# Down projection by Strassen's identity and softmax of two head groups at once, in a two-layer attention and GeGLU kernel

## The chip, the cores and the metric

The kernel runs on one core of a Trainium2 chip. A core has five engines that run their own instruction lists and meet at semaphores: TensorE (PE) for matrix products, with its weight loads (PEld) beside them, VectorE (DVE), ScalarE (ACT), GpSimd (POOL), and SyncE (SP), which here issues all DMA transfers. Matrix products land in PSUM, everything else is in SBUF. The metric is the time of one execution on the device in microseconds (us), the median of several runs.

## The reference

Two layers, each with the same weights: a dilated sliding-window attention and a GeGLU feed-forward network, both behind a layer norm and with a residual. Sequence S = 2048, width D = 512, 32 heads of 16, window W = 8 at dilation 2, F = 1792, all in float32.

```python
x = A_x
x = x + _A_ref(_layernorm(x), A_wqkv, A_wo)        # attention
x = x + _B_ref(_layernorm(x), w_gate, w_up, w_down)
x = x + _A_ref(_layernorm(x), A_wqkv, A_wo)
x = x + _B_ref(_layernorm(x), w_gate, w_up, w_down)

# attention: position p sees p, p-2, ..., p-14 of its own head
logits = einsum("bhsd,bhswd->bhsw", q, kg) * Dh**-0.5   # masked where p - 2w < 0
o = einsum("bhsw,bhswd->bhsd", softmax(logits), vg)
# feed-forward
y = (gelu(x @ w_gate) * (x @ w_up)) @ w_down
```

## The kernel before

Rows are split by parity, since a window of dilation 2 stays within one parity. A chunk is 256 rows of one parity, kept as J = 2 row tiles of 128; there are eight chunks a layer. For each chunk `attention_inputs` normalizes the rows and projects them to q, k and v (in two halves h of the heads, two row tiles j: four pieces of 24 matmuls, line 905), moves each piece from PSUM to a staging tile (line 925) and stores it to a DRAM tensor qkvd. `attention` fetches q, k and v back, with a halo of seven earlier rows so that a window is a shift along the free dimension, for four head groups of eight heads. Per head group VectorE multiplies the window of k by q (line 981), sums each product over 16 elements to logits (988), takes the softmax (1010 to 1034, exponential on ScalarE), multiplies the window of v by the weights in two instructions (1040) and adds the eight window places in a tree (1051 twice, 1056). `feed_forward` projects the result by wo, adds the residual, normalizes, and runs seven units u of two F blocks each: gate and up on TensorE into a PSUM tile pg (871), gelu on ScalarE (1141), product on VectorE (1149, called the eviction here: it frees the pg tile), and then the down projection (1174) into a PSUM tile pd.

Products of float32 are made of float16 halves: each operand is split into a high part and a remainder (`split`, `split_transpose`; the remainder of the gate product is GpSimd's line 1163, the cast ScalarE's 1158), and `passes` multiplies high by high, high by remainder and remainder by high. So each product is three matmuls. Weights are scaled by powers of two, which come from their largest absolute values (537, 547), before they are split (498 on VectorE, 514 and 518 on ScalarE and GpSimd).

The order of the work is laid out before the program is emitted. Every step is a node of a `Graph` with an engine, an estimated time, its reads and writes, and a priority; `plan` simulates the engines and takes the node that can start soonest, ties by priority. The priorities are built from the table of numbers `AT`. A `Lease` is the use of one buffer of a `Pool`; a node that gets a lease waits until a buffer is free. Before, pg has three buffers of two PSUM banks, pd one of two banks, the staging tiles three of their own. Once planned, each engine's list is fixed, and an engine that waits holds up everything behind it.

## Time and profile before

| what | us |
|---|---|
| median of 3 runs (lowest to highest) | 1263.62 (1263.05 to 1264.64) |
| span of the profiled execution, first to last instruction | 1259.6 |
| TensorE busy | 1229.9 (98%) |
| VectorE busy | 989.2 (79%) |
| ScalarE busy | 497.6 (40%) |
| GpSimd busy | 415.5 (33%) |

The page gives the profiled execution's span and no other time of its own; the span lies 4.0 us under the median of the runs. Busy time is the time in which an engine has an instruction under way. A group row of the profile has the line, the engine, the operation, output <- inputs, the shapes and the count, then the busy time in us and the mean of one in ns, then the engine's idle time ahead of such instructions and what ended it. A row of the chain or of the timeline has start and duration in us. A row of the table of windows has the window and its length, the busy time of each engine with its instructions, the granted TensorE clock (1.00 is full), the busy share of the DMA engines and GB/s.

### The profile page before, as it was taken

How to read it: one execution, taken by the hardware profiler on the slowest of the kernel's cores; microseconds unless marked ns; L12 is line 12 of the kernel's file. 1: busy time of each engine (PE TensorE's matmuls, PEld its weight loads, DVE VectorE, ACT ScalarE, POOL GpSimd, SP SyncE). 2: the span in 40 equal slices, each digit the busy share in tenths (PEclk: the TensorE clock that was granted, in tenths of full speed). 3: DMA queues.
4: the chain of work that ended last, by engine and by line, in shares of the span. 5: the costliest groups of instructions: out<-in, count | busy, mean ns of one | idle time of the engine just before them, and what ended most of it. 6: DMA issues, size and time to landing. Idle time of an engine off the chain costs nothing.

```text
span 1259.6 us, 21521 instructions
## 1 busy us (share of the span) xinstructions
PE 1229.9 (98%) x8714; PEld 854.8 (68%) x8714; DVE 989.2 (79%) x1422; ACT 497.6 (40%) x754; POOL 415.5 (33%) x405
## 2 busy tenths in 40 slices
PE   6988999999999999999999999999999999999998
PEld 3654585767767676767666667667676667776775
DVE  7989888988888889889888988688898888952011
ACT  6856383433434334343333343233343333321211
POOL 3523455252524243434233242332311314231211
PEclk8998999999999999999999999999999999999999
DMA  9999724735544543645282562835454463210000
GB/s 314 328 309 258 199 93 116 218 91 141 153 116 145 141 129 112 182 109 156 70 234 78 153 165 84 202 82 122 134 145 153 119 187 103 71 43 35 18 18 17
DMA packets 195779, 174.59 MB, mean 139 GB/s; under 512 B 101904, under 2 KB 162656, under 8 KB 195680
## 3 DMA queue, kind: packets, MB, share of 16 engines
q1 hardware_dynamic: 195680, 173.23, 48.3%
q8 instruction: 68, 1.11, 0.4%
q14 instruction: 31, 0.25, 0.1%
HBM read 115.87 MB, written 33.73 MB: 119 GB/s over the span
## 4 chain that ended last, share of the span: by engine, by line
PE 89%; DMA 4%; DVE 2%; ACT 2%; POOL 1%; SPq 1%; issue 1%; POOLq 0%; DVEq 0%; ACTq 0%
PE pg L871 52%; PE pd L1174 22%; PE pg L905 15%; DMA ax<-hl 2%; DMA bx<-hl 1%; DMA x<-in_A_x_dram 1%; DVE prod L1040 0%; SPq L834 0%; ACT w_q L493 0%; DMA qkvd<-stg 0%; DMA xa<-in_A_x_dram 0%; ACT xn L860 0%; POOL hl L829 0%; DVE prod L1051 0%; DMA ot<-hl 0%
## 5 line engine op out<-in xcount | busy, mean ns | idle before, releaser
L871 PE MATMUL pg<-bx,w_g 128*128 128x256 f16 x2688 | 330.1, 273 | 0.4 <-DMA bx<-hl 0.4
L871 PE MATMUL pg<-bx,w_u 128*128 128x256 f16 x2688 | 330.0, 273 | 0.0
L1163 POOL TENSOR_TENSOR gh<-g,gh 128x512 f16<-128x512 f32 x112 | 165.4, 1476 | 444.4 <-ACT gh L1158 425.1
L1174 PE MATMUL pd<-w_d,gh 128*128 128x512 f16 x1344 | 304.6, 379 | 0.6 <-POOL gh L1163 0.6
L871 PEld LDWEIGHTS <-w_g 128*128 128x128 f16 x2688 | 262.8, 98 | 47.2 <-issue 0.5
L871 PEld LDWEIGHTS <-w_u 128*128 128x128 f16 x2688 | 263.0, 98 | 30.5
L905 PE MATMUL pg<-w_q,ax 128*128 128x512 f16 (+1 forms) x1536 | 260.8, 331 | 16.5 <-DMA ax<-hl 12.4
L905 PEld LDWEIGHTS <-ax 128*128 128x128 f16 x1536 | 151.7, 99 | 124.0 <-DMA ax<-hl 12.9
L1174 PEld LDWEIGHTS <-gh 128*128 128x128 f16 x1344 | 131.5, 98 | 143.5 <-POOL gh L1163 1.0
L1149 DVE SCALAR_TENSOR_TENSOR g<-pg,small,g 128x512 f32<-128x512 f32 (+1 forms) x128 | 85.8, 681 | 169.3 <-ACT g L1141 164.3
L1141 ACT ACTIVATE g<-pg,small 128x512 f32<-128x512 f32 (+1 forms) x128 | 79.5, 634 | 267.6 <-PE pg L871 262.1
L1040 DVE TENSOR_TENSOR prod<-v,lg 128x1024 f32<-128x1024 f32 x128 | 168.0, 1338 | 1.1
L981 DVE TENSOR_TENSOR prod<-k,q 128x2048 f32<-128x2048 f32 x64 | 152.5, 2382 | 0.9
L1051 DVE TENSOR_TENSOR prod<-prod 128x1024 f32<-128x1024 f32 (+1 forms) x128 | 148.2, 1158 | 2.5
L988 DVE TENSOR_REDUCE lg<-prod 128x128 f32<-128x2048 f32 x64 | 145.9, 2280 | 1.0
L829 POOL TENSOR_TENSOR hl<-xn,hl 128x512 f16<-128x512 f32 x64 | 91.9, 1446 | 152.7 <-ACT hl L825 152.6
L829 POOL TENSOR_TENSOR hl<-o,hl 128x256 f16<-128x256 f32 x64 | 68.7, 1074 | 184.4 <-ACT hl L825 173.2
L1158 ACT CAST gh<-g 128x512 f16<-128x512 f32 x112 | 68.9, 616 | 85.5 <-DVE g L1149 83.1
L925 ACT ACTIVATE stg<-pg 128x768 f32<-128x768 f32 x64 | 51.8, 810 | 109.2 <-PE pg L905 107.3
L871 PE MATMUL pg<-w_o,ot 128*128 128x512 f16 x384 | 85.7, 379 | 0.1
L1141 ACT ACT_TABLE_LOAD x42 | 53.9, 1283 | 61.9 <-PE pg L871 61.5
L871 PEld LDWEIGHTS <-ot 128*128 128x128 f16 x384 | 37.5, 98 | 42.7 <-DMA ot<-hl 0.6
(84 smaller groups left out, 715.1 us busy)
## 6 DMA issues: line engine op xcount, KB each, us to landing
k<-qkvd SPq DMA_DIRECT2D x64, 576.0 KB, 4.4
v<-qkvd SPq DMA_DIRECT2D x64, 576.0 KB, 3.7
qkvd<-stg SPq DMA_DIRECT2D x64, 384.0 KB, 3.5
q<-qkvd SPq DMA_DIRECT2D x64, 128.0 KB, 2.1
x<-in_A_x_dram SPq DMA_DIRECT2D x9, 512.0 KB, 5.3
xs<-x SPq DMA_DIRECT2D x8, 512.0 KB, 3.8
xa<-xs SPq DMA_DIRECT2D x16, 256.0 KB, 6.2
x<-xs SPq DMA_DIRECT2D x8, 512.0 KB, 4.9
```

Source lines behind the costliest of these rows:

```text
L829: "POOL", t_pool(n), lambda: nc.gpsimd.tensor_sub(lo(), src(), hi()),
L871: nc.tensor.matmul(pt, a, b, start=i == 0, stop=i == n - 1)
L905: nc.tensor.matmul(pt[:, lo:hi], a[:, i // 2, kt], part(h * KT + kt)[:, lo:hi], start=(i, kt) == (0, 0), stop=(i, kt) == (2, KT - 1),)
L981: nc.vector.tensor_mul(pr, win, q.tile()[:, 0:J].unsqueeze(2).to_broadcast([P, J, W, P]))
L988: lambda lgv=lgv: nc.vector.tensor_reduce(lgv(), pr.rearrange("p j w (h d) -> p j w h d", d=DH), axis=AX.X, op=ALU.add),
L1040: lambda j=j, v=v, lg=lg: nc.vector.tensor_mul(prod[:, j].rearrange("p w (h d) -> p w h d", d=DH), v.tile()[:, j : j + W].rearrange("p w ( ...
L1051: lambda a=a, b=b: nc.vector.tensor_add(pr[:, :, 0:a], pr[:, :, 0:a], pr[:, :, a:b]),
L1141: lambda sel=sel, h=h, pg=pg, gt=gt: nc.scalar.activation(gt.tile()[:, sel, 0:N], pg.tile()[:, sel, 0:N], AF.Gelu_apprx_tanh, scale=cst["s ...
L1149: lambda sel=sel, h=h, pg=pg, gt=gt: nc.vector.scalar_tensor_tensor(gt.tile()[:, sel, 0:N], pg.tile()[:, sel, JM * P : JM * P + N], cst["c ...
L1158: lambda gt=gt, gh=gh: nc.scalar.copy(gh.tile()[:, 0, :, 0:N], gt.tile()[:, :, 0:N]),
L1163: lambda gt=gt, gh=gh: nc.gpsimd.tensor_sub(gh.tile()[:, 1, :, 0:N], gt.tile()[:, :, 0:N], gh.tile()[:, 0, :, 0:N]),
L1174: nc.tensor.matmul(pd.tile()[:, j], gh.tile()[:, a, i, cs], wd_of(f, b), start=f == 0 and n == 0, stop=f == NF - 1 and n == 2,)
```

## The change

The down projection takes a 2 x 2 x 2 block form: the two row tiles of a chunk, the two F blocks of a unit, and the two halves of D. Strassen's identity computes it with seven block products in place of eight, each 128 x 128 by 128 x 256, in three passes. For that the seven combinations of the gate blocks are made for every unit (`sums` on GpSimd), then cast and split, and the seven combinations of the w_down blocks are made once at the start (`finish`: sums and remainder on VectorE, cast on ScalarE). The seven products are accumulated over all units in seven blocks of 256 columns of a pd tile that is now four banks, and six VectorE instructions gather them into the rows. With pd grown, pg has two buffers of two banks; the two further ones that lie in pd's banks are withdrawn at the very start. Softmax is taken over two head groups in one instruction each; the weighted v is one multiplication and one reduction over the window, read with a stride of 128 elements, in place of two multiplications and the tree. The norm ahead of the feed-forward moves from VectorE's to GpSimd's form. Staging tiles, gate tiles, normalized rows and scratch share one pool sc of three buffers; k and v share one of three. The table of priorities is new.

On VectorE, around the first evictions of gate tiles (g in before, sc in after). In before:

```order
L1040 TENSOR_TENSOR prod<-v_108,lg_112 128x1024
L1051 TENSOR_TENSOR prod<-prod 128x2x512
L1051 TENSOR_TENSOR prod<-prod 128x2x256
L1056 TENSOR_TENSOR o_116<-prod 128x256
L1149 SCALAR_TENSOR_TENSOR g_117<-pg_126,small,g_117 128x512
L981 TENSOR_TENSOR prod<-k_105,q_109 128x2048
L1149 SCALAR_TENSOR_TENSOR g_118<-pg_128,small,g_118 128x512
```

and in after, where L703 to L706 are the sums and L728 the remainders of w_down:

```order
L1176 TENSOR_REDUCE o_112<-prod 128x256
L728 TENSOR_TENSOR w_d<-w_d 128x1792
L703 TENSOR_TENSOR sc_101<-sc_101 128x128
L704 TENSOR_TENSOR sc_101<-sc_101 128x256
L705 TENSOR_TENSOR sc_101<-sc_101 128x128
L706 TENSOR_TENSOR sc_101<-sc_101 128x128
L1275 SCALAR_TENSOR_TENSOR sc_102<-pg_122,small,sc_102 128x512
L1166 TENSOR_TENSOR prod<-kv_105,lg_109 128x2048
L1176 TENSOR_REDUCE o_112<-prod 128x256
L728 TENSOR_TENSOR w_d<-bx_96,w_d 128x7x128
L728 TENSOR_TENSOR w_d<-sc_100,w_d 128x7x128
L1275 SCALAR_TENSOR_TENSOR sc_102<-pg_123,small,sc_102 128x512
```

The w_down preparation, which was GpSimd's and ScalarE's, stands between attention and the first evictions.

On SyncE's queue, where the first chunk's q and k are fetched from qkvd. In before:

```order
L531 DMA w_u<-in_B_w_up_dram 128x896
L531 DMA w_g<-in_B_w_gate_dram 128x896
L936 DMA qkvd_64<-stg_104 128x6x128
L963 DMA q_109<-qkvd_64 128x256
L963 DMA q_110<-qkvd_64 128x256
```

and in after:

```order
L555 DMA w_u<-in_B_w_up_dram 128x896
L555 DMA w_d<-in_B_w_down_dram 128x512 x12
L831 DMA xa_89<-in_A_x_dram 128x512
L831 DMA xa_87<-in_A_x_dram 128x512
L788 DMA qkvd_65<-zeros 12x7x128 x2
L831 DMA xa_88<-in_A_x_dram 128x512
L1077 DMA q_106<-qkvd_64 128x256
```

Twelve of the fourteen w_down loads now stand ahead of the first fetch; in before all stood behind it.

On the same queue, the stores of projections shortly ahead of the first gate/up in after (stg_102, stg_103 and stg_104 took turns in before):

```order
L1047 DMA qkvd_64<-sc_102 128x6x128 x2
L831 DMA xa_88<-in_A_x_dram 128x512
L940 DMA_TRANSPOSE ax_92<-hl_99 128x8x128
L940 DMA_TRANSPOSE ax_94<-hl_98 128x8x128
L1047 DMA qkvd_64<-sc_102 128x6x128
L1077 DMA kv_105<-qkvd_64 128x1152
L1047 DMA qkvd_64<-sc_102 128x6x128
L940 DMA_TRANSPOSE ot_97<-hl_99 128x4x128
L1047 DMA qkvd_64<-sc_102 128x6x128
```

Thirteen stores in a row leave from the one buffer sc_102, while w_down's preparation and the gate tiles hold the others.

The diff, cut to its core:

```diff
 AT = dict(
-    lq0=-1380.0, lq1=-908.3, lf0=-0.8, lo=20.4, lf1=59.8, ld=93.7, pq0=-1380.0, pq1=-275.7, pf0=10.5, po=1.8,
...
+    lq0=-6486.17, lq1=-3733.04, lf0=-475.32, lo=-1195.16, lf1=-292.25, ld=-286.77, pq0=-1258.2, pq1=2564.18,
...
-    P_pg = pool("pg", 3, [P, 2, 512], F32, ps, fifo=False)
-    P_pd = pool("pd", 1, [P, JM, 512], F32, ps)
+    pd_all = ps.tile([P, 8, HD], F32, name="pd")
+    pd_two = pd_all.rearrange("p (t b m) c -> p t b (m c)", t=2, b=2)
+    P_pg = Pool("pg", [ps.tile([P, 2, 512], F32, name=f"pg{i}") for i in range(2)] + [pd_two[:, i] for i in range(2)], fifo=False)
+    P_pd = Pool("pd", [pd_all])
...
-    P_st = pool("stg", 3, [P, 3, HH, P])
...
+    P_sc = pool("sc", 3, [P, 7 * P], fifo=False)
...
+        def sums(b):
+            tt = (nc.gpsimd if AT["ds"] else nc.vector).tensor_tensor
+            tt(b[:, 0], b[:, 3], b[:, 6], op=ALU.add)
+            tt(b[:, 1:3], b[:, 3:7:2], b[:, 4:7:2], op=ALU.add)
+            tt(b[:, 4], b[:, 4], b[:, 6], op=ALU.subtract)
+            tt(b[:, 5], b[:, 5], b[:, 3], op=ALU.subtract)
...
+                lambda: g.add("ACT", t_act(7 * n), lambda: nc.scalar.copy(hi, blocks()), **rest[0]),
+                lambda: g.add(
+                    "POOL" if AT["dl"] else "DVE port", t_pool(7 * n) if AT["dl"] else t_dve(7 * n),
+                    lambda: sub(lo, blocks(), hi), **rest[1],
+                ),
...
+                def av(v=v, lg=lg, heads=heads):
+                    r = v.tile()[:, 0]
+                    win = bass.AP(r.tensor, r.offset, [r.ap[0], [P, J], [P, W], [DH, HPG], [1, DH]])
+                    nc.vector.tensor_mul(
+                        prod.rearrange("p j w (h d) -> p j w h d", d=DH), win,
+                        lg.tile()[:, :, :, heads].unsqueeze(4).to_broadcast([P, J, W, HPG, DH]),
+                    )
...
+                    lambda o=o: nc.vector.tensor_reduce(
+                        o.tile(), prod.rearrange("p j w c -> p j c w"), axis=AX.X, op=ALU.add
                     ),
...
-            for a, b in ((4, 8), (2, 4)):
-                g.add(
-                    "DVE port", t_dve(J * a * P),
-                    lambda a=a, b=b: nc.vector.tensor_add(pr[:, :, 0:a], pr[:, :, 0:a], pr[:, :, a:b]),
...
-        nl, sb_of = norm(xt, T - 1000)
-        bx = Lease(P_bx)
+        nl, sb_of = norm(xt, T - 1000, "POOL" if AT["fp"] else "DVE")
+        bx = Lease(P_bx, only=c % 2)
...
+                tt = nc.gpsimd.tensor_tensor if AT["sp"] else nc.vector.tensor_tensor
+                tt(b[:, 4:6], b[:, 0:2], b[:, 3:4].to_broadcast([P, 2, P]), op=ALU.add)
+                tt(b[:, 6], b[:, 0], b[:, 2], op=ALU.add)
+                tt(b[:, 1:3], b[:, 1:3], b[:, 0:4:3], op=ALU.subtract)
...
-                            nc.tensor.matmul(
-                                pd.tile()[:, j], gh.tile()[:, a, i, cs], wd_of(f, b),
-                                start=f == 0 and n == 0, stop=f == NF - 1 and n == 2,
-                            )
...
+                for m in ms:
+                    for n, (a, b) in enumerate(((0, True), (0, False), (1, True))):
+                        nc.tensor.matmul(
+                            pd.tile()[:, PD_AT[m]], gh_of()[:, a, G_AT[m]], wd_of(u, m, b),
+                            start=u == 0 and n == 0 and PD_AT[m] % 2 == 0,
+                            stop=u == NU - 1 and n == 2, skip_group_check=True,
+                        )
...
+        for to, of, sign in (
+            ((1, 2), (5, 4), 1), ((0, 3), (4, 3), 1), ((0, 3), (5, 2), -1), ((1, 2), (3, 2), 1),
+            ((0, 3), (7, 6), 1), ((0, 3), (1, 1), 1),
+        ):
```

More of the change, by code (lines that the diff above doesn't have):

```diff
@@ L1064, in attention @@
         return ot, mark
-    ts_ = {"store": None}
     def feed_forward(l, c, T, ot, mark):
@@ L1070, in feed_forward @@
         N = J * P
+        last = l == 1 and c == len(CHUNKS[l]) - 1
         xt, xl = load_x(l, c, T - AT["xl"], order=[mark])
@@ L1194, in feed_forward @@
-        last = l == 1 and c == len(CHUNKS[l]) - 1
+                "DVE", t_dvp(D), gather, r=[(pd, m) for m in {*of}], w=[(xl, j) for j in range(J)], prio=T - 2500,
+            )
         for js in [slice(j, j + 1) for j in range(J)] if last else [slice(0, J)]:
```

443 lines of the change are left out of this document (274 added, 169 removed).

## The prediction

> **What bounds the kernel now.** I read the busy shares and the chain that ended last first, then the same shares cut at the moment the first gate/up projection starts (154.5 us, a row of the chain further down).
>
> ```profile
> PE 1229.9 (98%) x8714; PEld 854.8 (68%) x8714; DVE 989.2 (79%) x1422; ACT 497.6 (40%) x754; POOL 415.5 (33%) x405
> PE 89%; DMA 4%; DVE 2%; ACT 2%; POOL 1%; SPq 1%; issue 1%; POOLq 0%; DVEq 0%; ACTq 0%
> ...
> core 0: us, PE busy (x) PEld busy (x) DVE busy (x) ACT busy (x) POOL busy (x), PEclk, DMA share, GB/s
> 0.00:52.53 52.53, 40.74 (x227) 23.76 (x228) 40.50 (x86) 38.20 (x58) 23.21 (x61) 0.94 0.94 321
> 0.00:154.47 154.47, 130.31 (x748) 75.66 (x749) 133.16 (x229) 93.65 (x151) 56.79 (x106) 0.93 0.95 283
> 154.47:1200.00 1045.53, 1044.97 (x7565) 739.80 (x7564) 847.85 (x1182) 394.71 (x588) 350.60 (x292) 1.00 0.44 124
> ```
>
> TensorE carries 89% of the chain. From 154.5 to 1200 us it is idle for 0.6 us of 1045.5 at full clock, so there the time is TensorE's list of work and nothing else. Before 154.5 us it idles 24 us and runs at a granted clock of 0.93, while VectorE (133 of 154 us) and the DMA engines (95%) are the full ones. So I make two sums: when the stream of gate/up projections begins, and how much TensorE work is left from there.
>
> What TensorE pays per matmul is read from unbroken pieces of the chain, not from the mean of one in the groups, since matmuls overlap.
>
> ```profile
> 154.47 15.72 PE pg L871 x144
> ...
> 280.94 5.18 PE pd L1174 x24
> ...
> 291.36 7.80 PE pg L905 x48
> 299.16 5.24 PE pg L871 x48
> ```
>
> A 256-column matmul takes 5.24/48 = 109.2 ns, a 512-column one 5.18/24 = 215.8 ns. The third piece (24 of each) confirms both: 24 x 0.325 = 7.80. After 154.5 us, 1259.6 - 154.5 = 1105.1 us follow.
>
> **The change part by part.** *Down projection.* Per pair of F blocks, 12 matmuls of 512 columns become 7 products x 3 passes = 21 of 256: 12 x 0.2158 = 2.59 us becomes 21 x 0.1092 = 2.29 us. Gate/up already runs one weight load and 256 columns per matmul, so the new form has a price in the trace. 16 chunks x 7 pairs x 0.297 = **-33.3 us**, all of it on TensorE's path. (The eighth product that Strassen saves is 12.5%; a 256-column matmul costs 1.2% more than half a 512-column one.) The Trainium skill ("TensorE: Matmul & The Clock Gate", Back-to-back issue gap) says streams of load-and-matmul pairs are spaced at about 131 ns for 512 columns and 81 ns for 128; by that, halving columns would lose: 1344 x 0.131 = 176 us before against at least 2352 x 0.081 = 191 us after, slower by 15 us or more. The rows above (215.8 and 109.2 ns) contradict it, so it gets no chance.
>
> *Order of TensorE.* 96 projection matmuls (four pieces of 3.9 us, 15.6 us) move ahead of the first gate/up. The total is the same; left from the first gate/up on are 1105.1 - 33.3 - 15.6 = 1056.2 us in before's terms, its tail included.
>
> *VectorE ahead of the first eviction.* There are only two gate/up buffers (pg) instead of three, so the third gate/up waits for the first eviction (L1149, now L1275). Before, it began here:
>
> ```profile
> 52.53 2.28 DVE L981 TENSOR_TENSOR prod<-k,q 128x2048 f32<-128x2048 f32 x1
> ...
> 160.47 0.75 DVE L1149 SCALAR_TENSOR_TENSOR g<-pg,small,g 128x512 f32<-128x512 f32 x1 [0.51 <-ACT g L1141]
> ...
> L1040 DVE TENSOR_TENSOR prod<-v,lg 128x1024 f32<-128x1024 f32 x128 | 168.0, 1338 | 1.1
> L981 DVE TENSOR_TENSOR prod<-k,q 128x2048 f32<-128x2048 f32 x64 | 152.5, 2382 | 0.9
> L988 DVE TENSOR_REDUCE lg<-prod 128x128 f32<-128x2048 f32 x64 | 145.9, 2280 | 1.0
> L1051 DVE TENSOR_TENSOR prod<-prod 128x1024 f32<-128x1024 f32 x64 | 90.1, 1408 | 1.1
> ...
> L1051 DVE TENSOR_TENSOR prod<-prod 128x512 f32<-128x512 f32 x64 | 58.1, 907 | 1.3
> L1056 DVE TENSOR_TENSOR o<-prod 128x256 f32<-128x256 f32 x64 | 32.6, 509 | 10.2 <-POOL hl L829 6.8
> ...
> L1010 DVE TENSOR_REDUCE mx<-lg 128x16 f32<-128x128 f32 x64 | 23.8, 372 | 0.8
> L1187 DVE SCALAR_TENSOR_TENSOR x<-pd,small,x 128x512 f32<-128x512 f32 x32 | 22.5, 746 | 19.2 <-PE pd L1174 19.2
> ...
> L1034 DVE TENSOR_TENSOR lg<-lg,mx 128x128 f32<-128x128 f32 x64 | 22.4, 361 | 0.1
> ...
> L791 DVE TENSOR_TENSOR nw<-nw 128x2 f32<-128x2 f32 x48 | 7.7, 161 | 1.1
> ```
>
> The new order puts ahead of that eviction: five full units of the w_d preparation (three sums of 256, one of 512, one subtraction of 1792: 3 x 0.51 + 0.91 + 2.1 = 4.5 us each, the 2.1 read between L1051's 1024 and L981's 2048), and three half units without their subtraction (1.6 us each): +27.5 us. Attention: eight q-k products and reductions instead of six (+9.3), four paired softmaxes at about 2.8 us instead of six single at 2.1 (-1.4), seven weighted sums instead of six. A weighted sum was 2 x 1.34 + 1.41 + 0.91 + 0.51 = 5.5 us; now it is one multiplication (2.38, L981) and one reduction of 2048 elements. If the reduction takes L988's 2.28, that is 7 x 4.66 against 6 x 5.5 (-0.4). The norm's 13 small steps go to GpSimd (-2.1). Sum +33 us: the first eviction begins at 160.5 + 33 = 193.5 and ends at about 194.
>
> That reduction is the unknown. It reads one element every 512 bytes; L988 reads side by side. Lower bound 2.28 us. The nearest strided reduction is L1010, which steps 32 bytes: 372 ns for 128 elements. Side by side, the next fence has 1076 ns for 896, so with L988 a slope of (2280 - 1076)/1152 = 1.045 ns and a start of 140 ns; L1010 then has (372 - 140)/128 = 1.81 ns an element, and 2048 of those would be 3.85 us. I take the lower end, because L1010 is a short instruction over three dimensions and its 98 ns may be a fixed cost; L988 is nearest in size. The upper end is the first rival.
>
> ```profile
> L537 DVE TENSOR_REDUCE small<-w_u 128x1 f32<-128x896 f32 x8 | 8.6, 1076 | 0.4 <-DMA w_u<-in_B_w_up_dram 0.4
> ...
> L1163 POOL TENSOR_TENSOR gh<-g,gh x112: 1153/1164/3198, 162.1 to 1251.7; 128x512 f16<-128x512 f32 x112
> ...
> L829 POOL TENSOR_TENSOR hl<-o,hl x64: 667/708/2344, 78.5 to 1124.1; 128x256 f16<-128x256 f32 x64
> ...
> 466.10 1.34 POOL L1163 TENSOR_TENSOR gh<-g,gh 128x512 f16<-128x512 f32 x1 [1.42 <-ACT gh L1158]
> 466.46 3.13 DVE L981 TENSOR_TENSOR prod<-k,q 128x2048 f32<-128x2048 f32 x1
> ...
> qkvd<-stg SPq DMA_DIRECT2D x8, 384.0 KB, 4.4
> ...
> qkvd<-stg SPq DMA_DIRECT2D x7, 384.0 KB, 2.6
> ...
> L925 ACT ACTIVATE stg<-pg 128x768 f32<-128x768 f32 x64 | 51.8, 810 | 109.2 <-PE pg L905 107.3
> ...
> L518 POOL TENSOR_TENSOR w_d<-w_d 128x512 f16<-128x512 f32 x14 | 18.2, 1301 | 10.6 <-ACT w_d L514 10.6
> L804 POOL TENSOR_TENSOR nw<-nw,root 128x2 f32<-128x2 f32 (+1 forms) x17 | 16.8, 990 | 1.2
> ```
>
> *DMA order.* Twelve w_d loads (3.1 MB, at the first window's 321 GB/s 9.8 us) now stand ahead of the first k fetch on SP's queue, so attention starts near 62 instead of 52.5 us. I cost this at nothing: about ten weight splits and maxima at about 1.1 us each (L537's size) moved ahead of it too and cover it; were that late, up to 10 us.
>
> *After the first eviction.* The first down waits for the sums, cast and remainder of the first gate tile. GpSimd: 256-element operations at 0.71 us and 512 at 1.16 (medians) give 1.78 ns an element, so the three sums are 0.71 + 0.48 + 0.71 = 1.9 us and the 896-element remainder 1.85 us instead of 1.16; with the cast on ScalarE (0.9 us, by L925's 0.81 for 768) about 5 us, under the third gate/up's 5.2. Two microseconds for what sticks out. TensorE, finished with two gate/ups near 180 us, idles some 16 us. A 9.9 us wait at 99 us (waited for: ax) stands between the slices at granted clocks of 0.85 and 0.89, which cost 20 x (0.15 + 0.11) = 5 us of work; I add 3.
>
> ```profile
> 80.00:100.00 20.00, 10.13 (x65) 6.12 (x63) 18.04 (x30) 14.44 (x27) 11.62 (x19) 0.85 1.04 292
> 100.00:120.00 20.00, 20.00 (x109) 11.03 (x108) 19.72 (x27) 13.57 (x28) 4.73 (x3) 0.89 1.06 290
> ...
> 447.64 2.75 PE L1174 MATMUL pd<-w_d,gh 128*128 128x512 f16 x12
> 447.89 1.28 ACT L1141 ACT_TABLE_LOAD   x1 [3.24 <-PE pg L871]
> ...
> 449.91 0.75 DVE L1149 SCALAR_TENSOR_TENSOR g<-pg,small,g 128x512 f32<-128x512 f32 x1 [0.59 <-ACT g L1141]
> ...
> 1252.88 2.33 PE L1174 MATMUL pd<-w_d,gh 128*128 128x512 f16 x10 [0.55 <-POOL gh L1163]
> 1255.26 1.41 DVE L1187 SCALAR_TENSOR_TENSOR x<-pd,small,x 128x512 f32<-128x512 f32 x2 [4.38 <-PE pd L1174]
> ```
>
> *Steady state.* VectorE: attention 64 x (11.9 - 10.5) = -89 us, six gathers of 0.746 instead of two +48, the norm -34, w_d +34: about 948 us, still under TensorE. GpSimd: 112 x (3.75 - 1.16) = +290, 16 norms of eight small steps +63 (half of 16 x 8 x L804's 0.99, the longest of them), w_d -18: about 750 us, a share of 60%. GpSimd and VectorE's two-input operations exclude each other (466.46: a 2.29 us product takes 3.13, until the remainder that began at 466.10 has ended); but with the add tree gone VectorE issues about three such operations per head group instead of eight, so I take this as even, and leave 3 us of stalls. With two buffers an eviction must end within the next gate/up's 5.24 us; at 447.6 to 450.7 it took 3.0 with a table load. The halved table loads (84 to 54 in the order) save ScalarE time that nobody waits for.
>
> *End.* The last down is followed by six gathers in place of two additions; the last pieces of down are cut so that four run under TensorE: +1.5 us.
>
> *Sum.* The third gate/up starts near 197 (194, and 3 for waits on the way); left are 1056.2 - 10.5 for the two done = 1045.7. 197 + 1045.7 + 2 + 3 + 3 + 1.5 = 1252.2 us of span, less 2 for the idle microseconds and late tail already inside the 1105.1: 1250. Median and span differ by 1263.6 - 1259.6 = 4.0: **1254 us**, 0.8% faster. Two thirds of the gain are given back at the start.
>
> **Rivals.** *The strided reduction is slow.* For: L1010. Against: nothing of its size. The Trainium skill ("Advanced Engine Details and Errata", SBUF Cachelines) says that accesses which each go to another 16-byte line pay a penalty, without a figure; L1010's extra 98 ns agrees in sign. At 3.85 us, eight reductions ahead of the second eviction add 13 us at the start, where VectorE leads: 1254 + 13 = 1267 us, slower. Over the kernel it adds 64 x 1.57 = 100 us, and VectorE at 1050 us would stay just below TensorE. It decides from 1.0 us extra per reduction on (3.3 us).
>
> *The staging buffer is the bound at the start.* Thirteen consecutive projections go through one staging buffer (shown in the order). Each takes 0.81 us of eviction, about 0.4 of issue and the store's landing, 2.6 us in a quieter stretch, 4.4 under load: 3.8 to 5.6 us against TensorE's 3.9. TensorE's first gate/up is at 154.5 + 15.6 + 0 to 22 = 170 to 192 and the third at 181 to 203, about hidden by VectorE; if stores take 6 us (7.2 a turn) it starts at 223: 1268 in the middle, up to 1280.
>
> *Two gate/up buffers and a fuller GpSimd make TensorE wait all along.* At 0.3 us for each of 112 gate/ups: 34 us, 1288. Against it is the 3.0 us above.
>
> **How the numbers follow.** Chances: the forecast 0.57 (its own range 1241 to 1261), slow reduction 0.25, staging 0.10, steady waits 0.08. The low end is a VectorE start 8 us earlier with no wait and no cold clock; the high end takes in the first two rivals: 1240 to 1277. A difference under 0.2% (1261.1 to 1266.1) can't be told from no change. Faster: 0.57 x 0.94 + 0.02 + 0.03 = 0.58. Same: 0.03 + 0.25 x 0.35 + 0.02 = 0.13. Slower: the rest, 0.29.
>
> **What the profile after would show.** Right: 21 down matmuls in 2.29 us; TensorE idle before the third gate/up with VectorE named, and dense after it; the first eviction between 190 and 200 us; the new reduction (L1176) near 2.28 us. Wrong: L1176 at 3 us or more; projections 5 us apart before the first gate/up; idle TensorE on evictions beyond 300 us.

## The result, and the profile after

The changed kernel takes 1321.2 us (median of 4 runs, 1314.6 to 1324.9) against 1263.6: a ratio of 1.0448 (95% interval 1.0419 to 1.0477). Forecast was 1254. The profiled execution has a span of 1318.7 us, where the working had 1250: 68.7 us to be found.

Busy shares and the chain that ended last, of after:

```profile
PE 1218.3 (92%) x9722; PEld 957.6 (73%) x9722; DVE 1090.7 (83%) x964; ACT 490.5 (37%) x691; POOL 799.6 (61%) x855
PE 32%; DVE 30%; POOL 19%; issue 8%; DMA 7%; ACT 4%; SPq 1%; POOLq 0%; DVEq 0%; ACTq 0%
```

TensorE had 89% of the chain before and has 32% now; VectorE and GpSimd together have 49%. No engine is full by its share of busy time. The piece of the chain in which the first gate/up begins, and from TensorE's timeline the end of the second gate/up and the start of the third:

```profile
193.47 5.25 PE pg L979 x48
...
202.48 1.47 PE L979 MATMUL pg<-bx,w_u 128*128 128x256 f16 x12
203.79 1.47 PE L979 MATMUL pg<-bx,w_g 128*128 128x256 f16 x12
```

The third follows the second at the usual step of 1.31 us: TensorE does not wait for the first eviction (200.80 us). The table of windows, cut where the first gate/up begins:

```profile
0.00:193.47 193.47, 151.41 (x844) 85.22 (x845) 178.09 (x235) 115.20 (x180) 75.58 (x119) 0.91 0.84 248
193.47:1260.00 1066.53, 1017.36 (x8434) 828.75 (x8432) 899.39 (x711) 364.47 (x497) 699.14 (x711) 0.99 0.41 118
```

TensorE was idle for 0.6 of 1045.5 us in this part of the kernel before; now it idles 49 of 1066.5 up to 1260 us. The third gate/up starts at 203.8 us, where 197 was forecast, and from there to the end 1114.9 us pass in place of 1053. So 7 us of the 68.7 are the start and 62 the rest. What TensorE waited for, of after (total, times, longest):

```profile
PE pd L1310 <- DVE x L1337: 28.0, 16, 5.6
PE pg L979 <- DVE sc L1275: 13.1, 8, 4.8
PE pg L1016 <- DMA ax<-hl: 11.3, 3, 7.2
PE pg L979 <- DMA ot<-hl: 10.0, 7, 2.6
```

Downs wait for the gathers (L1337), which read the one pd tile; gate/ups wait for evictions (L1275); the projection by wo waits for attention (ot). These three, of the four rows, end at VectorE or behind it. Its instructions, one by one (shortest, median, longest in ns):

```profile
L1176 DVE TENSOR_REDUCE o<-prod x64: 3567/3704/3777, 95.5 to 1217.0; 128x256 f32<-128x2048 f32 x64
...
L1100 DVE TENSOR_TENSOR prod<-kv,q x64: 2225/2291/3970, 62.0 to 1182.5; 128x2048 f32<-128x2048 f32 x64
...
L1131 DVE TENSOR_REDUCE mx<-lg x32: 554/583/601, 77.0 to 1188.8; 128x32 f32<-128x256 f32 x32
...
L1286 POOL TENSOR_TENSOR sc<-sc x112: 718/728/2789, 201.6 to 1300.2; 128x256 f32<-128x256 f32 x112
```

The strided reduction takes 3.70 us, where I had taken 2.28: with the start of 140 ns from the prediction, (3704 - 140)/2048 = 1.74 ns an element. And two-input operations are stretched: a product by up to 1.7 us, a GpSimd sum of 0.73 us by up to 2.1. What the two engines take turns at is called the port here. One such meeting, of after:

```profile
504.39 2.26 DVE L1166 TENSOR_TENSOR prod<-kv,lg 128x2048 f32<-128x2048 f32 x1
504.46 2.77 POOL L1286 TENSOR_TENSOR sc<-sc 128x256 f32<-128x256 f32 x1 [2.19 <-DVE nw L859]
506.75 3.75 DVE L1176 TENSOR_REDUCE o<-prod 128x256 f32<-128x2048 f32 x1
507.19 0.46 POOL L1287 TENSOR_TENSOR sc<-sc 128x128 f32<-128x128 f32 x1
507.73 0.73 POOL L1288 TENSOR_TENSOR sc<-sc 128x256 f32<-128x256 f32 x1
```

The sum begun at 504.46 ends 0.6 us after the product; beside the reduction the next two run at their usual length. The distributions say the same: the reductions hardly vary, the two-input operations do. The Trainium skill ("SBUF — State Buffer", Who interferes with whom) says that a reduction never contends with GpSimd on this chip, and that a two-input operation does; these rows agree.

How a late VectorE reaches TensorE, in the timeline around 870 us of after:

```profile
859.47 2.77 POOL L1286 TENSOR_TENSOR sc<-sc 128x256 f32<-128x256 f32 x1
...
863.49 0.94 ACT L1296 CAST gh<-sc 128x896 f16<-128x896 f32 x1 [5.95 <-POOL sc L1288]
...
864.33 0.68 ACT L1267 ACTIVATE sc<-pg,small 128x512 f32<-128x512 f32 x1
...
865.12 0.75 DVE L1275 SCALAR_TENSOR_TENSOR sc<-pg,small,sc 128x512 f32<-128x512 f32 x1 [3.47 <-ACT sc L1267]
...
865.78 0.74 DVE L1337 SCALAR_TENSOR_TENSOR x<-pd,small,x 128x512 f32<-128x512 f32 x1
866.44 3.75 DVE L1176 TENSOR_REDUCE o<-prod 128x256 f32<-128x2048 f32 x1
...
870.11 0.74 DVE L1337 SCALAR_TENSOR_TENSOR x<-pd,small,x 128x512 f32<-128x512 f32 x1
870.26 0.41 ACT L931 CAST hl<-o 128x256 f16<-128x256 f32 x1 [0.99 <-DVE o L1176]
870.58 0.69 ACT L1267 ACTIVATE sc<-pg,small 128x512 f32<-128x512 f32 x1
870.77 2.62 DVE L1166 TENSOR_TENSOR prod<-kv,lg 128x2048 f32<-128x2048 f32 x1
...
873.31 0.74 DVE L1337 SCALAR_TENSOR_TENSOR x<-pd,small,x 128x512 f32<-128x512 f32 x1
873.97 0.73 DVE L1275 SCALAR_TENSOR_TENSOR sc<-pg,small,sc 128x512 f32<-128x512 f32 x1
874.63 2.18 DVE L1337 SCALAR_TENSOR_TENSOR x<-pd,small,x 128x512 f32<-128x512 f32 x3
876.86 3.43 PE L1310 MATMUL pd<-w_d,gh 128*128 128x256 f16 x17 [4.57 <-DVE x L1337]
```

The six gathers of a chunk have a strided reduction, a product and an eviction between them. The gelu is done at 871.27, its eviction waits 2.7 us in VectorE's list, and the next chunk's first down, which needs the pd tile, waits 4.57 us for the last gather. ScalarE's list hands delays on as well: the gelu at 864.33 stands behind a cast that waited 5.95 us for GpSimd's sums (the first of them stretched to 2.77 us), the one at 870.58 behind a cast that waited for the strided reduction.

### The profile page after: what moved, and what is told of

Its sections match the earlier page's. It is cut to its first block, busy times and chain, and to the rows that moved or that the text cites. A ratio compares the mean times of both kernels' runs of the same rounds, so it can differ in the third digit from the quotient of the medians.

```text
span 1318.7 us, 23744 instructions
## 1 busy us (share of the span) xinstructions
PE 1218.3 (92%) x9722; PEld 957.6 (73%) x9722; DVE 1090.7 (83%) x964; ACT 490.5 (37%) x691; POOL 799.6 (61%) x855
## 4 chain that ended last, share of the span: by engine, by line
PE 32%; DVE 30%; POOL 19%; issue 8%; DMA 7%; ACT 4%; SPq 1%; POOLq 0%; DVEq 0%; ACTq 0%
PE pg L979 17%; DVE o L1176 8%; PE pd L1310 8%; PE pg L1016 6%; DVE prod L1166 4%; POOL sc L1286 4%; DVE prod L1100 4%; POOL hl L935 3%; DVE x L1337 3%; DVE lg L1109 3%; POOL sc L1287 2%; POOL sc L1288 2%; POOL w_u L1301 2%; POOL w_g L1301 2%; POOL gh L1301 1%
## 5 line engine op out<-in xcount | busy, mean ns | idle before, releaser
L979 PE MATMUL pg<-bx,w_g 128*128 128x256 f16 x2688 | 331.7, 273 | 13.2 <-DVE sc L1275 13.1
L979 PEld LDWEIGHTS <-w_u 128*128 128x128 f16 x2688 | 263.5, 98 | 31.0
L1176 DVE TENSOR_REDUCE o<-prod 128x256 f32<-128x2048 f32 x64 | 236.9, 3702 | 18.1 <-POOL hl L935 16.8
L1275 DVE SCALAR_TENSOR_TENSOR sc<-pg,small,sc 128x512 f32<-128x512 f32 (+1 forms) x128 | 85.4, 677 | 134.1 <-ACT sc L1267 134.0
L1286 POOL TENSOR_TENSOR sc<-sc 128x256 f32<-128x256 f32 x112 | 122.3, 1092 | 96.3 <-DVE sc L1275 93.8
L1100 DVE TENSOR_TENSOR prod<-kv,q 128x2048 f32<-128x2048 f32 x64 | 165.0, 2577 | 3.0 <-DMA kv<-qkvd 2.7
L1166 DVE TENSOR_TENSOR prod<-kv,lg 128x2048 f32<-128x2048 f32 x64 | 163.1, 2548 | 0.6
L1267 ACT ACTIVATE sc<-pg,small 128x512 f32<-128x512 f32 (+1 forms) x128 | 79.3, 631 | 95.6 <-PE pg L979 91.8
L1310 PE MATMUL pd<-w_d,gh 128*128 128x256 f16 x798 | 97.4, 278 | 13.3 <-DVE x L1337 13.3
L1310 PE MATMUL pd<-w_d,w_u 128*128 128x256 f16 x777 | 93.7, 276 | 11.9 <-DVE x L1337 11.6
L1310 PEld LDWEIGHTS <-gh 128*128 128x128 f16 x798 | 79.5, 100 | 25.5 <-issue 14.5
L1288 POOL TENSOR_TENSOR sc<-sc 128x256 f32<-128x256 f32 x112 | 91.5, 817 | 8.8
L1310 PEld LDWEIGHTS <-w_u 128*128 128x128 f16 x777 | 76.9, 99 | 24.5 <-issue 12.5
L1310 PE MATMUL pd<-w_d,w_g 128*128 128x256 f16 x777 | 91.2, 272 | 3.2 <-DVE x L1337 3.1
```

Source lines behind the costliest of these rows:

```text
L979: nc.tensor.matmul(pt, a, b, start=i == 0, stop=i == n - 1)
L1100: nc.vector.tensor_mul(prod, win, q.tile().unsqueeze(2).to_broadcast([P, J, W, P]))
L1166: nc.vector.tensor_mul(prod.rearrange("p j w (h d) -> p j w h d", d=DH), win, lg.tile()[:, :, :, heads].unsqueeze(4).to_broadcast([P, J, W ...
L1176: lambda o=o: nc.vector.tensor_reduce(o.tile(), prod.rearrange("p j w c -> p j c w"), axis=AX.X, op=ALU.add),
L1275: lambda sel=sel, h=h, pg=pg, g_of=g_of: nc.vector.scalar_tensor_tensor(g_of()[:, sel], pg.tile()[:, sel, JM * P : JM * P + N], cst["c_up" ...
L1286: tt(b[:, 4:6], b[:, 0:2], b[:, 3:4].to_broadcast([P, 2, P]), op=ALU.add)
```

## The experiments

Two theories at first. A: the strided reduction overloads VectorE. B: GpSimd's 800 us and the port that it shares with VectorE do it, or the gathers behind one pd tile. All times are medians; the change against after uses 1321.2.

**The stride alone.** The reduction reads side by side, its 2048 elements otherwise the same:

```diff
-    o.tile(), prod.rearrange("p j w c -> p j c w"), axis=AX.X, op=ALU.add
+    o.tile().rearrange("p j c -> p (j c)"),
+    prod.rearrange("p j w c -> p (j w c)").rearrange("p (n w) -> p n w", w=W),
+    axis=AX.X, op=ALU.add
```

> Kernel after, every instruction in its place; only the reduction of the weighted values reads each group of eight elements side by side instead of 512 bytes apart (so it sums other elements: the output is not attention). Theory A, the strided read is what carries the loss: the reduction falls from 3.70 us to about 2.28, VectorE loses 64 x 1.42 = 91 us of work, and the time falls from 1321 to 1250 to 1272 us. Rival B, the loss sits in GpSimd's 800 us and the port that it shares with VectorE, or in the six gathers behind one pd tile: the reduction falls as said, the time stays at 1295 us or more.

Measured: 1265.9 us, 55 less; 1.0024 of before (1.0010 to 1.0037). From the page of the contiguous run:

```profile
PE 1203.6 (95%) x9722; PEld 953.0 (75%) x9722; DVE 981.7 (78%) x964; ACT 488.0 (39%) x691; POOL 802.4 (64%) x855
PE 76%; DVE 8%; POOL 7%; DMA 5%; issue 2%; ACT 2%; SPq 0%; POOLq 0%; ACTq 0%; DVEq 0%
...
L1176 DVE TENSOR_REDUCE o<-prod 128x256 f32<-128x2048 f32 x64 | 145.8, 2278 | 18.9 <-POOL hl L935 17.5
```

and from its chain and its waits:

```profile
185.46 15.72 PE pg L979 x144
```

```profile
PE pd L1312 <- DVE x L1339: 12.5, 13, 2.8
```

The stride costs 1.42 us a time, 91 us of VectorE, and 55 us of the 57.6 between the two kernels. 8 of them lie before the third gate/up (195.8 instead of 203.8), 47 behind. Theory A holds, but B was not excluded by it:

**GpSimd's sums alone.** The stride stays, the sums go.

```diff
-    tt(b[:, 4:6], b[:, 0:2], b[:, 3:4].to_broadcast([P, 2, P]), op=ALU.add)
-    tt(b[:, 6], b[:, 0], b[:, 2], op=ALU.add)
-    tt(b[:, 1:3], b[:, 1:3], b[:, 0:4:3], op=ALU.subtract)
+    tt(b[0:1, 4:7, 0:1], b[0:1, 0:3, 0:1], b[0:1, 0:3, 0:1], op=ALU.add)
```

> Kernel after without GpSimd's seven-block sums of every gate tile (three operations of 128 to 256 elements, 112 times, replaced by one of three elements, so that the products of the sums are wrong); the strided reduction stays. GpSimd loses some 112 x 2 = 220 us and VectorE the collisions with them. Theory A, the strided reduction carries the loss: 1295 us or more. Rival B: 1280 us or less.

In the runs without sums GpSimd also clears the three sc tiles once at the start (2.5 us), and 112 operations of three elements stay, 0.66 us each.

Measured: 1273.3 us, 48 less: B's number, against A. Page of the run without sums:

```profile
PE 1208.4 (95%) x9722; PEld 955.5 (75%) x9722; DVE 1050.3 (82%) x964; ACT 490.6 (39%) x691; POOL 582.6 (46%) x634
```

Neither theory holds alone: either relief brings most of the loss back. TensorE hardly waits for GpSimd itself, 2.4 us in after. But without the sums its waits for gathers fall from 28.0 to 9.7 us, for evictions from 13.1 to 6.4, for attention from 10.0 to 2.1; VectorE is busy for 40 us less, and ScalarE's waits for the sums fall from 356 to 138 us. So GpSimd acts through the stretched instructions of VectorE, through ScalarE's list, or through both; no run separates these. Without the stride and the sums:

> The contiguous run with GpSimd's sums of the gate blocks left out too (one operation of three elements in their place): the two changes that took 55 and 48 us off when each was made alone. Theory A with the port as its second half, that VectorE's list with its collisions is one bound under which TensorE's list lies: the two gains do not add, the time stops at TensorE's floor, 1246 to 1256 us. Rival, two independent costs: 1215 to 1230 us.

Measured: 1257.0 us, 9 below the contiguous run and 1 above the range expected. 55 and 48 do not add; the loss is one bound, made by VectorE and GpSimd together, and TensorE's list lies under it.

**What the port is worth.** Two runs that change what holds the port. First the three additions of before in the reduction's place:

```diff
-    nc.vector.tensor_reduce(o.tile(), prod.rearrange("p j w c -> p j c w"), axis=AX.X, op=ALU.add)
+    nc.vector.tensor_add(prod[:, :, 0:4], prod[:, :, 0:4], prod[:, :, 4:8])
+    nc.vector.tensor_add(prod[:, :, 0:2], prod[:, :, 0:2], prod[:, :, 2:4])
+    nc.vector.tensor_add(o.tile(), prod[:, :, 0], prod[:, :, 1])
```

> Kernel after with the three additions of the kernel before (1024, 512 and 256 elements) in the place of the strided reduction, every other instruction where it was; the output is the reference's. The three took 1.41 + 0.91 + 0.51 = 2.83 us in the kernel before against 3.70 for the reduction: VectorE loses 64 x 0.87 = 56 us of work, but the three are two-input operations and meet GpSimd at the port. Theory A: 1265 to 1290 us. Rival B (GpSimd and the port): no gain, 1305 to 1330 us, since the additions come to stand in GpSimd's way.

Measured: 1316.6 us, 5 less: B's range, and not A's. Then the stride moved from the reduction's reads to the product's writes:

```diff
+    def turned():
+        flat = prod.rearrange("p j w c -> p (j w c)")
+        return flat.rearrange("p (j c w) -> p j w c", j=J, w=W)
...
-    prod.rearrange("p j w (h d) -> p j w h d", d=DH), win,
+    turned().rearrange("p j w (h d) -> p j w h d", d=DH), win,
...
-    o.tile(), prod.rearrange("p j w c -> p j c w"), axis=AX.X, op=ALU.add
+    o.tile(), turned().rearrange("p j w c -> p j c w"), axis=AX.X, op=ALU.add
```

> Kernel after, every instruction in its place; the product of weights and v is written with the eight window places side by side (each written element 32 bytes from the one before), so that the reduction reads side by side and its output is the reference's. The stride moves from the reduction's reads to the product's writes. If a strided write costs what a strided read costs (1.74 instead of 1.045 ns an element), the product goes from 2.29 us at its shortest to about 3.7 and the time stays at 1310 to 1325 us; if a strided write is free, the product stays at 2.29, the reduction at 2.28, and the time is that of the contiguous run, 1262 to 1272 us.

Measured: 1338.9 us, 18 more than after and outside both ranges. Page of the run with the additions:

```profile
PE 1218.5 (93%) x9722; PEld 956.7 (73%) x9722; DVE 1039.3 (79%) x1092; ACT 486.7 (37%) x691; POOL 860.7 (65%) x855
```

and page and distribution of the run with the strided write:

```profile
PE 1226.8 (92%) x9722; PEld 960.4 (72%) x9722; DVE 1085.7 (81%) x964; ACT 487.3 (36%) x691; POOL 879.3 (66%) x855
...
L1170 DVE TENSOR_TENSOR prod<-kv,lg x64: 3847/3890/5445, 93.4 to 1229.7; 128x2048 f32<-128x2048 f32 x64
```

A strided write costs somewhat more than a strided read: 3890 against 2292 ns, 0.78 ns an element, where the reduction has 0.70 (3704 against 2278). Both runs have VectorE less busy than after's 1090.7 us, and gain 5 us or lose 18. GpSimd's list is the same, yet its busy time grows from 800 to 861 and 879 us: it waits at the port inside its instructions. Estimates, with every share taken as proportional: by the contiguous run a microsecond of reduction is worth 55/91 = 0.6. The strided write trades 91 us of it for 98 on the port (L1166's 163.1 became 260.8); it loses 18 where 55 were to be gained, so a microsecond on the port is worth 73/98 = 0.75. By the additions, which trade 237 for 198: (237 x 0.6 - 5)/198 = 0.7. That the 55 and 48 us do not add says that such prices hold near after alone. Measured without them is that strided reduction and additions are about even in after (1321 and 1317 us); that the reason is a port freed by the one and filled by Strassen's sums fits these runs and is not shown by itself.

**The gathers.** Five of the six left out, in after and in the contiguous run:

```diff
     def gather(to=to, of=of, sign=sign):
+        if of != (1, 1):
+            return
```

> Kernel after with only the last of the six additions that gather the products of the down projection into the rows (five of six left out of the output); the strided reduction stays. VectorE loses 16 x 5 x 0.743 = 59 us of work, which does not meet GpSimd at the port, and TensorE the waits of each chunk's first down for the last gather (28 us in the profile of after). Theory A, VectorE is the engine that is waited for and one of its microseconds without the port is worth the 0.6 us of the contiguous run (55 us for 91): 36 us, to 1280 to 1290. Rival, the waits of TensorE on the one pd tile are a cost beside it: 60 us or more, to 1260 or below. Rival B, GpSimd sets the pace: 1305 or more.

> The contiguous run (1265.9 us, not attention) with only the last of the six gathers. There TensorE still waited 12.5 us for gathers behind the one pd tile, of some 14 us that it lay above the forecast from its third gate/up on. If the gathers are what was left out of the forecast, the time falls to 1249 to 1256 us; if the rest is GpSimd and the port, it stays at 1261 or more.

Measured: 1303.2 (18 less, where A said 31 to 41) and 1251.9 (14 less than contiguous). In after, 58 us less of VectorE are worth 0.3 each: TensorE's waits for gathers fall from 28.0 to 7.4, those for attention rise from 10.0 to 19.9.

```profile
PE pg L979 <- DMA ot<-hl: 19.9, 7, 5.4
...
PE pd L1310 <- DVE x L1339: 7.4, 4, 3.5
```

In the contiguous run the gathers are what I had left out: without five of them TensorE waits for no gather any more, and the time lies 2 us from the forecast's 1254. The 9 us that the sums are worth there overlap with this in part: without the sums the waits for gathers are 9.3 in place of 12.5 us. Eleven of the thirteen waits for gathers in the contiguous run are of this form, from its timeline:

```profile
251.39 1.47 PE L1312 MATMUL pd<-w_d,gh 128*128 128x256 f16 x12
252.91 0.75 DVE L1339 SCALAR_TENSOR_TENSOR x<-pd,small,x 128x512 f32<-128x512 f32 x1
253.71 1.14 PE L1312 MATMUL pd<-w_d,gh 128*128 128x256 f16 x9 [0.84 <-DVE x L1339]
```

The last down of a chunk is cut into four pieces so that gathers can begin between them. TensorE does not go on with the next piece until a gather that was begun has read the pd tile: 0.84 us, eleven times; the other two, 2.76 and 0.50 us, are a first down waiting for the last gather.

**One part alone, in the kernel before.** Only the strided reduction, in place of its additions:

```diff
-    lambda a=a, b=b: nc.vector.tensor_add(pr[:, :, 0:a], pr[:, :, 0:a], pr[:, :, a:b]),
+    lambda: None,
...
-    lambda o=o: nc.vector.tensor_add(o.tile()[:, 0:J], pr[:, :, 0], pr[:, :, 1]),
+    lambda o=o: nc.vector.tensor_reduce(
+        o.tile()[:, 0:J], pr.rearrange("p j w c -> p j c w"), axis=AX.X, op=ALU.add
+    ),
```

> Kernel before with only the strided reduction (256 sums over eight elements 512 bytes apart) in the place of its three additions, every other instruction where it was. VectorE gains 64 x 0.87 = 56 us, from 989 to 1045 us of 1260, without any of the other changes. Theory A in its strong form, that the reduction alone makes VectorE the engine that is waited for: 1280 us or more. Theory A in its weak form, that it needs the fuller VectorE and GpSimd of the changed kernel too: 1264 to 1275 us. Rival B: no change, within 3 us of 1263.6.

Measured: 1279.2 us, 1.0133 (1.0118 to 1.0149): between the strong and the weak form. VectorE goes from 989 to 1041.7 us. From its page, and the piece of its chain in which the first gate/up begins:

```profile
PE 1231.4 (96%) x8714; PEld 853.7 (67%) x8714; DVE 1041.7 (82%) x1294; ACT 499.1 (39%) x754; POOL 398.0 (31%) x405
PE 79%; DVE 10%; DMA 5%; POOL 2%; ACT 2%; issue 1%; SPq 0%; POOLq 0%; DVEq 0%; ACTq 0%
...
163.94 15.72 PE pg L871 x144
```

At 82% busy and with three pg tiles, VectorE already has 10% of the chain. Of the 18.2 us by which the span grows, 9.5 lie ahead of the first gate/up (163.9 us, 154.5 in before); behind it, from 170 to 1200 us, TensorE idles 7.9 us, where it idled 0.6 in a like stretch of before. That busy share is no slack.

**The order.** Rival C: the lists were laid out for a reduction of 2.29 us.

```diff
-    "DVE", t_dve(J * W * P),
+    "DVE", 3.7,
...
-    norm=359.9, proj=149.42, half=24.02, row=-49.66, att=87.48, ...
+    norm=258.16, proj=2053.71, half=-8.78, row=180.28, att=282.82, ...
```

> Kernel after with the strided reduction, the planner told its measured 3.70 us in place of 2.29, and its priorities searched anew under that cost (the old ones give an order that the planner puts at 1340 us, the new ones 1287); the computation and the output are the reference's. Theory A, that VectorE's work and the port are too much whatever the order: 1295 to 1325 us. Rival C, that the loss comes from an order laid out for a reduction of 2.29 us: 1270 or less.

Measured: 1311.3 us, 10 less, in A's range. VectorE is about as busy in this run (1080.4 us) and GpSimd too (802.0), and C explains 10 us; that a longer search finds more is not excluded.

**What sets the start.** The contiguous run's first eviction begins at 193.0 us, and my forecast was 193.5, for the reason of VectorE's work ahead of it. Against that reason stands its own trace: VectorE sits idle for 1.85 us ahead of this eviction, until the gelu is done, and TensorE's first three gate/ups are one unbroken piece of the chain (144 matmuls, 15.72 us). To test the reason, VectorE's sums and remainders of w_down were left out (all on top of the contiguous run):

```diff
-    tt(b[:, 0], b[:, 3], b[:, 6], op=ALU.add)
...
+    tt(b[0:1, 0:3, 0:1], b[0:1, 3:6, 0:1], b[0:1, 3:6, 0:1], op=ALU.add)
...
-    lambda: sub(lo, blocks(), hi), **rest[1],
+    lambda: nc.vector.memset(lo, 0.0), **rest[1],
```

> The contiguous run with VectorE's part of the w_down preparation left out (sums of three elements, remainders set to zero: the down projection is then another one). VectorE has some 22 us less ahead of the first eviction. If VectorE sets the start, as the forecast has it, the first eviction moves from 193 to 168 to 175 us, the third gate/up to 178 to 186, and the time to 1246 to 1257 us. If the projections behind the staging buffers set it, the first eviction stays at 188 or later and the time at 1262 or more.

In this run and in the later ones without w_down's preparation, GpSimd also clears four tiles once at the start (4.3 us).

Measured: 1267.7 us, first eviction at 198.1, with VectorE idle for 7.3 us ahead of it. The reason was wrong; why the eviction comes 5 us later is not shown. Then the stores on another queue, alone and with that:

```diff
-    (nc.scalar if AT["put"] else nc.sync).dma_start(d, staged()...
+    nc.scalar.dma_start(d, staged()...
```

> The contiguous run with the 64 stores of projections issued from ScalarE's queue in place of SyncE's, at the same places of the order. In its chain of waits the last projections ahead of the first gate/up hang on a transposed input (L940) that stands on SyncE's queue behind a store (L1047) which waits for the one staging buffer: 155.8 to 171.9 us, in which TensorE idles some 6 us and its clock falls to 0.83. If that queue sets the start, the first gate/up moves from 185 to 176 to 181 us and the time to 1255 to 1262. If the round trip of the staging buffer itself sets it (eviction, store, eviction), the time stays at 1263 to 1268.

> The same, and VectorE's part of the w_down preparation left out as in the run that gave 1267.7 us. If VectorE stands right behind the queue at the start, it now gains 5 to 12 us over the run with the stores alone; if neither is what TensorE waits for, the two agree within 3 us, and the start is bound by the chain of projections itself.

Measured: 1267.5 and 1267.9 us, first gate/up at 185.0 and 185.4: SyncE's queue does not set the start, alone or with w_down's preparation. Then a second staging tile, with and without w_down's preparation, and in after itself:

```diff
-    staged = lambda stg=stg: stg.tile()[:, 0 : 3 * HH * P]
+    def staged(stg=stg, mine=mine):
+        if not mine:
+            turns.append(0)
+            other = len(turns) % 2 and not begun
+            mine.append(P_gh.tiles[2].bitcast(F32)[:, 0 : 7 * P] if other else stg.tile())
+        return mine[0][:, 0 : 3 * HH * P]
```

> The contiguous run, and until the first gate tile is cast the staging tile of every other projection is the third gh tile, which nothing uses before that; every instruction keeps its place. If the round trip of the one staging buffer sets the start, the 6 us that TensorE idles between 160 and 180 go, the first gate/up moves from 185 to 172 to 180 us and the time to 1253 to 1262. If VectorE's work sets it, the first eviction stays at 191 or later and the time at 1263 to 1268.

> The same with VectorE's part of the w_down preparation left out as in the run of 1267.7 us. If both stand equally late, each hiding the other, now and only now the start moves: first gate/up at 170 to 176, time 1248 to 1256, and at least 5 us below the run with the second staging buffer alone. If TensorE's own projections are the floor, it agrees with that run within 3 us.

> Kernel after with the second staging tile alone; the computation and the output are the reference's. With the reduction at 3.70 us VectorE is busy for 97 of the 100 us up to 200, and from there on the pace is VectorE's: 1315 to 1325 us, no change. If the start counts in full, some 8 us less: 1309 to 1314.

Measured: 1265.3, 1264.1 and 1320.8 us; first gate/up at 187.4, 186.9 and 191.7. The round trip is gone from the chain and the start has not moved. Its chain now shows TensorE at work:

```profile
42.71 1.00 DVE small L561
...
53.96 1.87 DVE w_q L522 x2
...
73.20 20.00 PE pg L1025 x122
93.20 7.25 DMA ax<-hl
100.50 26.64 PE pg L1025 x161
...
187.56 15.72 PE pg L979 x144
```

From 73 us to the first gate/up TensorE is busy for 104.9 of 114.2 us. What is late, it seems, is the start of that stretch, the second chunk's projections, behind VectorE's maxima and remainders of w_gate and w_up (L561, L522, from 39 to 56 us). Those shortened:

```diff
-    dst, raw, axis=AX.X, op=ALU.max, apply_absolute_value=True
+    dst, raw[:, 0:64], axis=AX.X, op=ALU.max, apply_absolute_value=True
...
-    lambda: nc.vector.scalar_tensor_tensor(lo, raw, su, hi, op0=ALU.mult, op1=ALU.subtract),
+    lambda: nc.vector.memset(lo, 0.0) if w.key in "gu" else ...
```

> The contiguous run with VectorE's maxima of weights (L561, 1.08 us each, 15 of them between 20 and 70 us) taken over 64 elements in place of 768 or 896, and the remainders of w_gate and w_up set to zero in place of computed (L522, 1.1 us and more, ten of them there): some 20 us less of VectorE's work ahead of the second chunk's statistics. Scales and remainders are then others, the output is not the reference's. If that stretch sets the start, the projections of the second chunk begin at 50 to 58 us in place of 70, the first gate/up at 166 to 177 in place of 185, and the time falls to 1246 to 1258 us. If TensorE's start hangs on the loads or on the staging and transposes behind it, the first gate/up stays at 182 or later and the time at 1261 or more.

Measured: 1263.2 us, first gate/up at 182.4: 3 us. SyncE's queue in this run shows what is next:

```profile
37.62 7.87 SPq L557 DMA_DIRECT2D w_d<-in_B_w_down_dram  x12
45.79 1.02 SPq L833 DMA_DIRECT2D xa<-in_A_x_dram  x2
```

The second chunk's rows (xa) stand behind twelve w_down loads. So those were moved back, each to just ahead of its first use, alone and with every other suspect relieved:

```diff
+    for n in order:
+        if n not in loads:
+            late += sorted(before_of.get(n, []), key=place.get) + [n]
+    order = late
```

> The run with the short maxima, and each of the fourteen w_down loads issued just ahead of the instruction that first needs it, so that the second chunk's rows are loaded ahead of most of them. If the loads stand next behind VectorE, the second chunk's projections begin 5 to 10 us earlier than at 67 us, the first gate/up at 170 to 178 and the time at 1248 to 1259. If not, first gate/up 180 to 184 and 1260 to 1266 us.

> The same with the second staging buffer and without VectorE's part of the w_down preparation: every suspect at the start relieved at once. If several stand equally late, the start moves now if at all: first gate/up at 165 to 175 us, time 1243 to 1255. If it is bound by TensorE's own projections and the transposes ahead of them, it stays at 178 or later and 1257 us or more.

Measured: 1280.6 and 1277.3 us, 17 and 14 worse, the first outside both ranges; first gate/up at 201.4 and 198.7. A likely reason is in the waits of ScalarE between 40 and 90 us in the first of them:

```profile
ACT sc L575 <- DMA w_d<-in_B_w_down_dram: 15.9, 5, 4.8
```

ScalarE's magnitudes of w_down (L575) stand ahead of the second chunk's rows in its list and now wait 15.9 us for the loads; TensorE's waits ahead of 200 us for ScalarE to empty projections into staging tiles (L1040) are 14.4 us, where the run with the short maxima had 3.4. What sets the start stays open. Shown is that w_down's preparation, the stores' queue, the staging tile and the maxima are worth 3 us at most, one at a time, and that the loads must be early as long as ScalarE reads them where it does; moving loads and ScalarE's reads back together was not tried. For the 68.7 us between the forecast span and the measured one the start matters little: the third gate/up comes 7 us later than forecast in after and 1 us earlier in the contiguous run, and after does not gain from a second staging tile. Against before it costs about what was forecast: the first gate/up of after comes 39 us later, 15.6 of them projections moved ahead.

## Why the prediction was wrong

Two of the signs of being wrong that I had named appear: L1176 takes 3.70 us, and of the 13.1 us that TensorE waits for evictions 12.8 lie beyond 300 us.

*Down projection, -33.3 us.* Right: 21 matmuls take 2.29 us throughout (L1310, L1312).

*Projections moved ahead, 15.6 us.* The first gate/up of after, 193.5, lies beyond 170 to 192; that of the contiguous run, 185.5, within. The working went on with 170 ("finished with two gate/ups near 180"), the low end.

*VectorE ahead of the first eviction, 193.5.* The number was met where the reduction took the assumed 2.28 us (193.0), by luck: 22 us less of VectorE's work did not bring the eviction forward, and the 16 us that TensorE was to idle ahead of the third gate/up do not occur, in after or in the contiguous run. The projections came later than I took them, by about as much as I gave VectorE.

*"I take the lower end, because L1010 is a short instruction."* This step failed. The row that I set aside, 1.81 ns an element, was the right one (1.74 measured); its 98 ns were no fixed cost but the stride. The first rival had the mechanism, and was mis-sized: I gave it 13 us, at the start alone; it costs 55, 47 of them behind the start.

*"VectorE at 1050 us would stay just below TensorE."* This is why the rival was mis-sized. It compares a sum of busy times with a span. The sum itself came to 1090.7 us; 23 of the 41 beyond 1050 are the two large products of attention, which take 2.56 us on average in place of 2.38. VectorE also sits still for the next tile to evict, is stretched at the port, and keeps an eviction behind a 3.7 us instruction when one comes due. In before 1042 us cost 16 already, some half of it ahead of the first gate/up.

*"I take this as even", VectorE against GpSimd at the port.* Failed: fewer two-input operations on VectorE do not even out 290 us more on GpSimd. GpSimd's sums are worth 48 us beside the strided reduction, and 9 without it.

*Six gathers, +48 us of VectorE.* The size was right; TensorE's waits for them were left out. "The last pieces of down are cut so that four run under TensorE" was wrong: TensorE stops for each one that is begun there. Five of the six gathers are worth 14 us in the contiguous run, where its eleven stops make 9.2 us and I had 3 us of stalls in all.

*Cold clock, 3 us.* Its 5 us take TensorE as busy for all of the slice from 80 to 100 us; the row has 10.1 us, which makes 3.7.

*DMA order, nothing.* Attention starts at 62.0 us in after (L1100), as forecast. What that costs was not measured by itself; moving the loads back cost 17 us.

*Staging as the bound.* Not the cause by itself: a second tile moves nothing. *Two pg buffers and a fuller GpSimd, 34 us*: right in kind for the stretch behind the first gate/up, with the strided reduction as the half it lacked. I had the rivals as alternatives, each against an otherwise undisturbed kernel, and none above 1288 us. They were one bound with two sources, and came together.

## What to carry to other kernels

A reduction that reads with a stride is costed at the strided rate, by the nearest strided row, however short that is. An engine's list has to fit with its waits, not by its busy sum: where VectorE and GpSimd both fill up, add up what holds their port, ask what stands ahead of the instruction that frees a buffer, and let rivals that load the same bound occur together. And a number that comes out as forecast is no proof of its reason: take the reason away and see whether the number moves.

## What the runs showed of the hardware

A VectorE reduction of float32 takes 1.74 ns an element with a step of 512 bytes (2048 elements, 3704 ns) and 1.73 with one of 64 bytes (256 elements, 583 ns, L1131), against 1.045 side by side: between 64 and 512 bytes the step's size made no difference. The Trainium skill ("Advanced Engine Details and Errata", SBUF Cachelines) has a penalty for going to another 16-byte line with each access, and no figure. These rows agree and give 0.7 ns an element; no run here has a step that stays within a line. A two-input product that writes with a step of 32 bytes pays 0.78 ns an element more, and GpSimd's busy time grows by 80 us beside it, so in this kernel the reads of a reduction are the cheaper place for a stride: 1321 against 1339 us.
